# 512-column gate/up products for the first 1024 tokens with their result kept in DRAM, two down chunks per step, and a sixth seven-product unit in the sequence transform

## The chip, the cores and the metric

The kernel runs on one core of a Trainium2 chip. The metric is the device time in microseconds (us) of one execution, the median over several runs. The core has five engines that run beside one another, each with its instructions in a fixed order: TensorE (PE) multiplies, with its weight loads (PEld) overlapping; VectorE (DVE), ScalarE (ACT) and GpSimd (POOL) do elementwise work; SyncE (SP) issues the DMA transfers. An engine that waits for a semaphore holds back everything behind it in its own order.

## What is computed

One FNet block and one gated GELU block, on 2048 tokens of width 448, with a hidden width of 1792:

```python
# _A_ref: DFT over the hidden and the sequence axis, real part
a = jnp.einsum("bsd,ed->bse", x, dft_hid_re)
b = jnp.einsum("bsd,ed->bse", x, dft_hid_im)
y = jnp.einsum("ts,bse->bte", dft_seq_re, a) - jnp.einsum("ts,bse->bte", dft_seq_im, b)
...
# _B_ref
h = _gelu(g) * u            # g = x @ w_gate, u = x @ w_up
return jnp.einsum("bsf,fd->bsd", h, w_down)
...
h = x + _A_ref(_layernorm(x, axis=-1), A_dft_seq_re, A_dft_seq_im, A_dft_hid_re, A_dft_hid_im)
h2 = h + _B_ref(_layernorm(h, axis=-1), B_w_gate, B_w_up, B_w_down)
```

## The kernel before

Every operand of a product is split into two fp16 parts, a high one (written by ACT, line 106) and a low one (the rest, written by DVE, lines 110 and 112), and a product takes three terms: high by high, low by high, high by low. Many products are done by schemes with seven products of half size instead of eight; these need sums of operand blocks, which DVE or POOL make.

**Sequence transform, 0 to about 347 us.** The 16 token tiles are normalised in pairs, turned by DMA or PE, and multiplied by the hidden DFT (the feature matmuls F0 to F15, 22 of 448 columns each, into two PSUM banks `ab`, which ACT empties as the high part of `b` and DVE as the low part). Then come 8 passes p over 8 units u, each unit a block of the sequence DFT against two token tiles. A plain unit is 24 matmuls of 448 columns; a seven-product unit (its number is in `S_UNITS`) is 42 of 224 columns. The weights of a unit are loaded (`wr`), split into `ws` (`seq_parts`), and for a seven-product unit four sums are made (`wsum`: lines 518, 520 and 522, DVE) and split into `wss` (two buffers). Before, five units are of that kind and three plain.

The order on each engine in this stage is set when the kernel is built, by a planner: `arranged()` walks over tasks with a cost, a due time and the tasks they come after, and picks for each engine the earliest due task that is able to start. A table `SHIFT` moves due times by kind of task, `HOLD` lets an engine wait for a more urgent task, and `COST` has the length of a unit (plain 4.54, seven-product 4.02). Between these tasks lies the preparation of the gate/up weights: 14 groups f, each loaded (`gu_raw`), summed, split (`gu_p`) and stored to DRAM (`w_dram`). Groups in `LATE` (three before) are prepared later, during gate/up. The pass results are added to x and kept as h; layernorm of h and the operand sums of gate/up (`hops`) for the four quarters of 512 tokens follow in the same stage and beyond.

**Gate/up and down, 347 us to the end.** The tokens are in quarters of 512. A step t is one quarter q by one weight group f. With `TQ` = 256 columns it has seven products, A11B11 and A12B21 into bank pX, S2T2, S3T3 and A22T4 into pY, S1T1 and S4B22 into pZ, 39 matmuls in all (line 1199). The methods of `GateUp` (`x_open`, `x_close`, `y_mid`, `y_close`, `z_open`, `z_close`, `c_last`) issue them with the elementwise work: DVE writes hidden(1) from pZ in `y_mid` (`plus`, line 1209), hidden(0) from pY in `y_close` and `c12` from pZ in `z_close`; in `c_last` ACT applies GELU to c12 and POOL multiplies it into hidden(1) (line 1276). `z_close` adds into the bank that the plus in `y_mid` has read, and so comes after it.

A down chunk d is 21 matmuls of 224 columns (line 1144) for a part of the hidden width and of the tokens. `dn_sums` makes its sums `dn_s` (POOL: lines 1290 and 1291, DVE: 1292; `DN_S` = 3 buffers), `dn_split` its high and low parts `dn_w`. Steps 0 to 13 (the first quarter) have no chunk; each of steps 14 to 55 has one; 14 more follow at the end. The hidden values hh of a quarter stay in SBUF.

What sets the order here is the loop over t as written; the order on each engine is that of the calls. Pools that are closed and opened again (`reuse_waits="tile"`) put a wait on the first write of a new tile, for all that still uses the old ones at its place.

Of the kernel before, what the change touches and what calls it, by code (L numbers as in the profile page):

```python
# [14 lines left out]
P = 128  # L15
# [18 lines left out]
def kernel(  # L34
# [57 lines left out]
    G.memset(eps_t, EPS / X_SC**2)  # L92

# [35 lines left out]

    def root(mv, tag, of=1):  # L130
# [191 lines left out]
    S_UNITS, WR_BUFS, WS_BUFS, WSS_BUFS, STAGE_BUFS = (3, 4, 5, 6, 7), 3, 3, 2, 2
# [5 lines left out]
    xt, xs, xT, norm_x = {}, {}, {}, {}  # L328
    x_pairs = x.rearrange("(u g p) d -> u p g d", g=2, p=P)
# [93 lines left out]
    wh_hi = ring.tile([P, 4, 2 * D], F16, tag="ops", bufs=2, name="wh_hi")  # L423
    wh_lo = ring.tile([P, 4, 2 * D], F16, tag="ops", bufs=2, name="wh_lo")
# [76 lines left out]
    def sums_high(i):  # L501
        t = bop[i] = dft.tile([P, 2, 7, HD], F16, name=f"b{i}")
# [12 lines left out]
    def seq_sums(p, u):  # L515
        r = wr[p, u]
        s = wsum[p, u] = dft.tile([P, 4, 2 * P], F32, tag="wsum", bufs=1, name=f"wsum{p}_{u}")
        V.tensor_add(s[:, 0:2], r[:, 1:2].to_broadcast([P, 2, 2 * P]), r[:, 0:4:3])
        yield
        V.tensor_add(s[:, 2], s[:, 1], r[:, 0])  # L520
        yield
        V.tensor_add(s[:, 3], s[:, 2], r[:, 2])  # L522
# [39 lines left out]
    PRODUCTS = [(0, 0, 2, 0), (1, 2, 0, 1), (6, 1, 0, 0), (2, 6, 1, 1), (4, 3, 2, 1), (5, 5, 3, 0), (3, 4, 3, 1)]  # L562
# [42 lines left out]
    def seq_out(p):  # L605
# [12 lines left out]
        for g, ps in enumerate((X, Y)):  # L618
            eg = e[:, 2 * g : 2 * g + 2].rearrange("p o d -> p (o d)")
# [10 lines left out]
    class Weights:  # L630
# [52 lines left out]
        def beat(self, k):  # L683
# [31 lines left out]
    for n, s in zip((1, 3, 4, 5, 7), S_UNITS):  # L715
        mixed.insert(n, s)
# [900 lines left out]
```

## Time and profile before

| | |
|---|---|
| runs | 704.88, 705.37, 705.43 us; median 705.37 |
| the profiled execution, first to last instruction (span) | 703.5 us |
| its instructions | 15378 |
| mean granted TensorE clock | 0.999 |
| DMA over the span | 139.74 MB, mean 199 GB/s |
| sequence transform | about 0 to 347 us |
| first quarter, steps 0 to 13 | 352 to 411 us |
| steps 14 to 55 | 411 to 675 us |
| last 14 chunks | from 675 us |

The profile is of one execution. The median of the runs lies 1.87 us above its span; changes are worked out on the span and carried over to the runs. "Busy" is the time in which an engine worked on instructions. For PE it is modelled and overlaps, so it says that PE had work, not how fast: for that, starts are compared. L12 is line 12 of the kernel.

### The profile page before, as it was taken

The page shows a single profiled execution, that of the slowest core. Times are in us where ns is not written, and L with a number is a line of the kernel's source. Part 1 is how long each engine was busy: PE and PEld are TensorE (multiplying, and loading weights), DVE is VectorE, ACT ScalarE, POOL GpSimd, SP SyncE. Part 2 cuts the span into 40 slices and gives each one's busy share as a digit, 9 for nine tenths or more (in the row PEclk, how much of TensorE's full clock was granted, in tenths as well). Part 3 has the DMA queues.
Part 4 walks back from the last instruction along what each step waited for, and adds up shares of the span by engine and source line. Part 5 has one row for each costly group of instructions (what it writes and reads, how often), then busy time and mean ns, then how long its engine had stood idle before and what let it go on. Part 6 is the DMA issues. An engine that isn't in the chain of part 4 may idle for free.

```text
span 703.5 us, 15378 instructions
## 1 busy us (share of the span) xinstructions
PE 697.0 (99%) x6046; PEld 584.1 (83%) x6046; DVE 563.2 (80%) x1170; ACT 408.0 (58%) x862; POOL 198.8 (28%) x225
## 2 busy tenths in 40 slices
PE   8999999999999999999999999999999999999998
PEld 5556578878787878778888889999999999999998
DVE  6999999999999897989578877575765755786786
ACT  5776674667576565656267765555555544455432
POOL 0000000000000000001136754474664745647342
PEclk9999999999999999999999999999999999999999
DMA  9554555687988867777579665658466594545401
GB/s 330 160 128 114 142 170 184 233 245 227 228 275 202 283 177 261 262 253 281 182 258 353 204 211 170 191 180 199 170 195 190 178 200 173 181 158 166 151 27 54
DMA packets 81849, 139.74 MB, mean 199 GB/s; under 512 B 41712, under 2 KB 59376, under 8 KB 81776
## 3 DMA queue, kind: packets, MB, share of 16 engines
q1 hardware_dynamic: 81776, 138.76, 63.5%
q8 instruction: 47, 0.77, 0.5%
q14 instruction: 26, 0.21, 0.1%
HBM read 109.25 MB, written 20.19 MB: 184 GB/s over the span
## 4 chain that ended last, share of the span: by engine, by line
PE 95%; DMA 1%; ACT 1%; DVE 1%; issue 1%; SPq 0%; ACTq 0%; DVEq 0%
PE acc L574 38%; PE acc_d L1144 15%; PE pY L1199 14%; PE pZ L1199 9%; PE pX L1199 9%; PE ab L457 9%; DMA x<-in_x_dram 1%; DVE dn_w L110 0%; ACT dn_w L106 0%; SPq L429 0%; ACT xn_h L254 0%; DVE st_x L354 0%; DVE hh L1209 0%; ACT wd L106 0%; ACT g L1252 0%
## 5 line engine op out<-in xcount | busy, mean ns | idle before, releaser
L1199 PEld LDWEIGHTS <-gw 128*128 128x128 f16 x2184 | 213.1, 98 | 23.7 <-issue 1.0
L574 PE MATMUL acc<-b,ws 128*128 128x224 f16 (+1 forms) x1296 | 204.6, 301 | 0.0
L574 PEld LDWEIGHTS <-ws 128*128 128x128 f16 x1296 | 125.6, 98 | 53.2
L1199 PE MATMUL pY<-hops,gw 128*128 128x256 f16 x952 | 129.1, 273 | 0.0
L1144 PE MATMUL acc_d<-wd,dn_w 128*128 128x224 f16 x1050 | 122.3, 259 | 0.0
L574 PE MATMUL acc<-b,wss 128*128 128x224 f16 x960 | 118.2, 259 | 0.0
L235 POOL TENSOR_TENSOR wd_s<-wd 128x448 f32<-128x448 f32 x7 | 10.1, 1442 | 346.8 <-DMA wr<-in_w_seq_dram 330.0
L1144 PEld LDWEIGHTS <-dn_w 128*128 128x128 f16 x1050 | 101.1, 98 | 2.9
L574 PEld LDWEIGHTS <-wss 128*128 128x128 f16 x960 | 92.3, 98 | 0.1
L106 ACT ACTIVATE ws<-wr 128x256 f16<-128x256 f32 (+2 forms) x104 | 62.4, 637 | 41.1 <-PE acc L574 16.1
L1199 PE MATMUL pZ<-hops,gw 128*128 128x256 f16 x616 | 85.5, 273 | 0.4 <-DVE hh L1209 0.3
L1276 POOL TENSOR_TENSOR hh<-hh,c 128x256 f32<-128x256 f32 x56 | 46.3, 828 | 139.7 <-ACT c L1274 139.5
L1199 PE MATMUL pX<-hops,gw 128*128 128x256 f16 x616 | 83.3, 273 | 0.0
L112 DVE SCALAR_TENSOR_TENSOR ws<-wr,ws 128x256 f16<-128x256 f32 (+2 forms) x104 | 70.6, 709 | 1.4 <-ACT ws L106 1.3
L110 DVE TENSOR_TENSOR dn_w<-hh,dn_w 128x256 f16<-128x256 f32 x50 | 25.3, 506 | 53.1 <-ACT dn_w L106 52.8
L106 ACT ACTIVATE wss<-wsum 128x1024 f16<-128x1024 f32 x40 | 42.1, 1053 | 36.8 <-DVE wsum L522 21.1
L457 PEld LDWEIGHTS <-xT 128*128 128x128 f16 x352 | 33.9, 98 | 32.8 <-ACT xT L420 1.5
L110 DVE TENSOR_TENSOR dn_w<-dn_s,dn_w 128x640 f16<-128x640 f32 x50 | 54.6, 1092 | 7.4 <-ACT dn_w L106 6.7
L1243 ACT ACTIVATE u<-pY 128x256 f32<-128x256 f32 x56 | 21.4, 382 | 61.4 <-PE pY L1199 61.3
L1291 POOL TENSOR_TENSOR dn_s<-hh 128x256 f32<-128x256 f32 x42 | 52.8, 1258 | 0.0
L112 DVE SCALAR_TENSOR_TENSOR wss<-wsum,wss 128x1024 f16<-128x1024 f32 x40 | 48.8, 1220 | 4.1 <-ACT wss L106 4.0
L1238 ACT ACTIVATE pY<-pX 128x256 f32<-128x256 f32 x56 | 20.6, 368 | 50.3 <-PE pX L1199 50.3
(120 smaller groups left out, 936.9 us busy)
## 6 DMA issues: line engine op xcount, KB each, us to landing
gw<-w_dram SPq DMA_DIRECT2D x53, 896.0 KB, 4.8
wr<-in_w_seq_dram SPq DMA_DIRECT2D x64, 512.0 KB, 4.4
gu_raw<-in_w_gu_dram SPq DMA_DIRECT2D x28, 384.0 KB, 4.8
w_dram<-gu_p SPq DMA_DIRECT2D x33, 256.0 KB, 3.1
hx<-in_x_dram SPq DMA_DIRECT2D x8, 448.0 KB, 4.5
h_dram<-hx SPq DMA_DIRECT2D x8, 448.0 KB, 4.8
hr<-h_dram SPq DMA_DIRECT2D x8, 448.0 KB, 5.3
x<-in_x_dram SPq DMA_DIRECT2D x7, 448.0 KB, 6.9
```

The source lines that it names most:

```text
L106: A.activation(dst, src, AF.Copy, scale=scale)
L110: V.tensor_sub(dst, src, hi)
L112: V.scalar_tensor_tensor(dst, src, scale, hi, op0=ALU.mult, op1=ALU.subtract)
L235: G.tensor_sub(s[:, 2:4], t[:, 0:2], t[:, 2:4])
L457: PE.matmul(feat[i][r][:, :D], xT[i][:, kx, :], w[:, kw, r * D : (r + 1) * D], start=n == 0, stop=n == 10,)
L574: PE.matmul(banks[k][:, cols], lhs, rhs, start=k not in begun, stop=stop, skip_group_check=True)
L1144: PE.matmul(acc[k // 2][:, k % 2 * HD : (k % 2 + 1) * HD], a_of(la, a), b_of(lb, b), start=first and m == 0 and k % 2 == 0, stop=last and ...
L1199: PE.matmul(ps, w[:, wl, wa + ws, :], ops[:, m + ms, :], start=first and n == 0, stop=last and n == len(terms) - 1, skip_group_check=True,)
L1238: A.activation(self.Y, self.X, AF.Copy)
L1243: A.activation(self.u2, self.Y, AF.Copy, scale=SC)
L1276: G.tensor_mul(c22, c22, self.c12)
L1291: E.tensor_sub(s[:, 2:4], t[:, 1:4:2], t[:, 0:4:2])
```

## The change

1. `S_UNITS` gets unit 2 as well: six seven-product units and two plain ones. The blocks of a seven-product unit are renumbered so that its three plain blocks lie side by side and `seq_parts` splits them as one piece of 768 columns instead of 256 and 512. In a pass the units come in the order 0, 2, 3, 4, 1, 5, 6, 7; before, 0, 3, 1, 4, 5, 6, 2, 7.
2. The moments of the token pairs u = 7 and 4 are made by ACT (`x_moments`), and for those and for h two small steps of the reciprocal root go to ACT (`half_of` and a square).
3. The table `SHIFT` and `HOLD` have new values, with more kinds, and `LATE` has six groups instead of three: {3: 0, 5: 4, 7: 8, 9: 12, 11: 16, 13: 20}.
4. Steps 0 to 13 take the first 1024 tokens at 512 columns. Their hidden values go to `hid` tiles (4 buffers, pool scr), are stored to `hid_dram` (`store`), and are loaded as `hid_in` (6 buffers) for chunks 0 to 27. Steps 14 to 27 and 28 to 41 take the third and fourth quarter at 256 columns; there are 42 steps instead of 56. `CHUNK_COUNT` gives the chunks of steps 14 to 41, two or one; 14 follow at the end as before.
5. The product of `c_last` is a call of its own (`c_mul`), on POOL, or on DVE in steps 15 to 28. Pools are laid out anew: hh2 lies in `later`, opened when `half0` (with scr and the hid tiles) is closed in step 14.

Cut to its core:

```diff
-    S_UNITS, WR_BUFS, WS_BUFS, WSS_BUFS, STAGE_BUFS = (3, 4, 5, 6, 7), 3, 3, 2, 2
+    S_UNITS, WR_BUFS, WS_BUFS, WSS_BUFS, STAGE_BUFS = (2, 3, 4, 5, 6, 7), 3, 3, 2, 2
+    BY_SCALAR = (7, 4)
...
-            return [(w[0], slice(0, 1), r[:, 0:1]), (w[0], slice(1, 3), r[:, 2:4])]
+            return [(w[0], slice(0, 3), r[:, 1:4])]
...
-    for n, s in zip((1, 3, 4, 5, 7), S_UNITS):
+    for n, s in zip((1, 2, 3, 5, 6, 7), S_UNITS):
         mixed.insert(n, s)
...
-    SHIFT = {"copy": -31.8, "fhigh": -68.2, "fhighp": -18.1, "flow": 9.9, "fsum": 12.9, "guhi": 1.2, "gulo":
+    SHIFT = {"copy": 3226.4, "fhigh": -1619.2, "fhighp": 1413.8, "flow0": -1035.9, "flow1": -969.5,
...
-    HOLD = (0.23, 17.8)
+    HOLD = (0.24, 56.3)
...
-    LATE = {4: 0, 8: 7, 12: 15}
+    LATE = {3: 0, 5: 4, 7: 8, 9: 12, 11: 16, 13: 20}
...
+    STEPS = [(0, f) for f in range(NF)] + [(2, f) for f in range(NF)]
+    STEPS += [(3, f // 2 + f % 2 * (NF // 2)) for f in range(NF)]
...
+            self.n = 4 * P if wide else TQ
...
+            if (self.t, g) not in hid:
+                hid[self.t, g] = scr.tile([P, 4 * P], F32, tag="hid", bufs=HID_BUFS, name=f"hid{self.t}_{g}")
+            return hid[self.t, g]
+
+        def store(self, g):
+            k, n = divmod(self.f, NC)
+            nc.sync.dma_start(hid_dram[n][:, :, k, g, :], hid[self.t, g].rearrange("p (j c) -> p j c", j=4))
...
+    HID_BUFS, IN_BUFS = 4, 6
...
+    def hid_load(d):
+        p, n = divmod(d, NC)
+        hid_in[d] = early.tile([P, 4, P], F32, tag="hid_in", bufs=IN_BUFS, name=f"hid_in{d}")
+        nc.sync.dma_start(hid_in[d], hid_dram[n][:, p].rearrange("p k g c -> p (k g) c"))
...
-    N_GU = 4 * NF
+    N_GU = 3 * NF
+    ops3 = []
+    CHUNK_COUNT = (2, 2, 2, 1, 2, 2, 2, 1, 2, 2, 2, 1, 2, 2) + (2, 1) + (2, 1, 1, 1, 1, 1) * 2
...
             prev.c_last()
+            if t == NF:
+                prev.c_mul()
+                for g in range(2):
+                    prev.store(g)
+                half0.close()
+                later = ctx.enter_context(tc.tile_pool(name="later", bufs=1, side="right", reuse_waits="tile"))
+                hh[2] = later.tile([P, NC, 4, TQ], F32, name="hh2")
```

**The order at the start, DVE.** The rows follow the statistics of token pair x10, x11; `wsum0_5` is the first sum of unit 5 in pass 0, `b0` and `b1` are the low parts of the first two feature tiles (`ab0_0` is a PSUM bank), DMAHW6 the landing of wr0_5. Before:

```order
45 L354 BN_STATS st_x4_393<-x2_376 128x6 [waits DMAHW2_49]
46 L354 BN_STATS st_x5_394<-x2_376 128x6 [waits DVE_49]
47 L356 BN_AGGR mv_x4_392<-st_x4_393 128x2 [waits DVE_49]
48 L356 BN_AGGR mv_x4_392<-st_x5_394 128x2 [waits DVE_49]
49 L112 SCALAR_TENSOR_TENSOR b0_345<-ab0_0_231,b0_345 128x448 [waits Activation_49]
50 L112 SCALAR_TENSOR_TENSOR b0_345<-ab0_1_232,b0_345 128x448 [waits Activation_49]
51 L518 TENSOR_TENSOR wsum0_5_403<-wr0_5_383 128x512 [waits DMAHW6_49]
52 L112 SCALAR_TENSOR_TENSOR b1_365<-ab1_0_280,b1_365 128x448 [waits Activation_49]
```

The same place on DVE in the changed kernel:

```order
45 L549 TENSOR_TENSOR wsum0_5_395<-wr0_5_384 128x512 [waits DMAHW6_49]
46 L369 BN_STATS st_x4_398<-x2_377 128x6 [waits DMAHW2_49]
47 L369 BN_STATS st_x5_399<-x2_377 128x6 [waits DVE_49]
48 L371 BN_AGGR mv_x4_397<-st_x4_398 128x2 [waits DVE_49]
49 L371 BN_AGGR mv_x4_397<-st_x5_399 128x2 [waits DVE_49]
50 L114 SCALAR_TENSOR_TENSOR b0_346<-ab0_0_232,b0_346 128x448 [waits Activation_49]
51 L114 SCALAR_TENSOR_TENSOR b0_346<-ab0_1_233,b0_346 128x448 [waits Activation_49]
52 L114 SCALAR_TENSOR_TENSOR b1_366<-ab1_0_281,b1_366 128x448 [waits Activation_49]
```

`wsum0_5` has moved from behind b0 to ahead of the statistics of x4 and x5.

**The order from step 13 to step 14, DVE.** Rows 752 to 763 of the changed kernel; step 13 is the last wide one, and hh2 in the last row is the first write to the place that the hid tiles had; DMAHW1, 2, 6 and 7 are there the landings of the four stores of hid12 and hid13:

```order
752 L1324 SCALAR_TENSOR_TENSOR hid13_0_5745<-pY_13_5615,g1_13_5693 128x512 [waits DMAHW3_49,PE_49]
753 L1258 SCALAR_TENSOR_TENSOR c12_13_5752<-pZ_13_5638,u2_13_5651 128x512 [waits PE_49,Pool_49]
754 L112 TENSOR_TENSOR dn_w0_5758<-hid_in0_5590,dn_w0_5758 128x256 [waits Activation_49]
755 L112 TENSOR_TENSOR dn_w0_5758<-dn_s0_5671,dn_w0_5758 128x640 [waits Activation_49]
756 L112 TENSOR_TENSOR dn_w1_5763<-hid_in1_5592,dn_w1_5763 128x256 [waits Activation_49]
757 L112 TENSOR_TENSOR dn_w1_5763<-dn_s1_5675,dn_w1_5763 128x640 [waits Activation_49]
758 L1361 TENSOR_TENSOR dn_s2_5768<-hid_in2_5667 128x128 [waits DMAHW4_49]
759 L1361 TENSOR_TENSOR dn_s3_5772<-hid_in3_5669 128x128 [waits DMAHW5_49,DVE_49]
760 L114 SCALAR_TENSOR_TENSOR wd_4627<-wd_s_6_5633,wd_4627 128x1120
761 L112 TENSOR_TENSOR dn_w2_5798<-hid_in2_5667,dn_w2_5798 128x256 [waits Activation_49]
762 L112 TENSOR_TENSOR dn_w2_5798<-dn_s2_5768,dn_w2_5798 128x640 [waits Activation_49]
763 L1258 SCALAR_TENSOR_TENSOR hh2_5787<-pZ_14_5725,u3_14_5829 128x256 [waits DMAHW2_49,DMAHW6_49,DMAHW1_49,DMAHW7_49,Activation_49,Pool_49]
```

At the same place before, between the first and second quarter, DVE had less ahead of that write:

```order
748 L1209 SCALAR_TENSOR_TENSOR c12_13_5508<-pZ_13_5415,u2_13_5428 128x256 [waits PE_49,Pool_49]
749 L112 SCALAR_TENSOR_TENSOR wd_4572<-wd32_6_5317,wd_4572 128x448 [waits DMAHW5_49,Activation_49]
750 L110 TENSOR_TENSOR dn_w1_5527<-hh0_4599,dn_w1_5527 128x256 [waits Activation_49]
751 L110 TENSOR_TENSOR dn_w1_5527<-dn_s1_5378,dn_w1_5527 128x640 [waits DVE_49,Activation_49]
752 L1209 SCALAR_TENSOR_TENSOR hh1_5516<-pZ_14_5482,u3_14_5550 128x256 [waits DMAHW3_49,DMAHW1_49,Activation_49]
```

The write of step 14 now stands behind three chunks' low parts instead of one, and waits for four transfers of step 12 and 13.

**The same place, POOL of the changed kernel.** The product that finishes hid13 (the last row, L1336) stands behind the sums of chunks 2 and 3; the DVE wait of dn_s3 is for a free dn_s buffer, which the low part of chunk 0 frees:

```order
49 L1336 TENSOR_TENSOR hid12_1_5628<-hid12_1_5628,c12_12_5665 128x512 [waits DMAHW2_49,Activation_49]
50 L1359 TENSOR_TENSOR dn_s2_5768<-hid_in2_5667 128x256 [waits DMAHW4_49]
51 L1360 TENSOR_TENSOR dn_s2_5768<-hid_in2_5667 128x256
52 L1359 TENSOR_TENSOR dn_s3_5772<-hid_in3_5669 128x256 [waits DMAHW5_49,DVE_49]
53 L1360 TENSOR_TENSOR dn_s3_5772<-hid_in3_5669 128x256
54 L1336 TENSOR_TENSOR hid13_1_5715<-hid13_1_5715,c12_13_5752 128x512 [waits DMAHW7_49,DMAHW0_49,Activation_49]
```

The store of hid13_1 on SP waits for that last row. Before, the product of a step was of 256 columns and nothing was stored behind it.

More of the change, by code (lines that the diff above doesn't have):

```diff
@@ L763, in chain @@
         for k, cost in enumerate(costs):
-            last = [add(engine, cost, due, lambda k=k: step(k == 0), after=last, kind=kind)]
+            on, cost = cost if isinstance(cost, tuple) else (engine, cost)
+            last = [add(on, cost, due, lambda k=k: step(k == 0), after=last, kind=kind)]
         return last[0]
@@ L1083 @@
     gu_late(min(LATE))
+    for n in range(2):
+        down_load(n)
     h_store(N_PASS - 1)
-    down_load(1)
     banks_dft.close()
@@ L1325, in dn_drain @@
     def dn_drain(p):
-        v = [ftile(f"v{k}", 1, f"v{k}_{p}", D) for k in range(2)]
+        v = fpool.tile([P, 2, D], F32, tag="v", name=f"v_{p}")
+        v = [v[:, k] for k in range(2)]
         return Drain(hr[p], acc_d[p], v, 1.0 / (H_SC * W_SC))
@@ L1471, with some @@
             cur.z_close()
[L1472 to L1474 removed]
+            if t >= 10:
+                for d in chunks(t + 3):
+                    hid_load(d)
+            for d in chunks(t + 1):
+                dn_split(d)
+            for d in chunks(t + 2):
+                dn_sums(d)
+            do(t, 2)
+            down_end(t)
             late_prep(2 * t + 1)
+            do(t, 4)
         else:
+            mms = [(d, k) for d in chunks(t) for k in range(21)]
+            def some(a, b):
+                n = len(chunks(t))
+                for d, k in mms[a * n : b * n]:
+                    dn_mm(d, range(k, k + 1))
             do(t, 0)
             prev.c_last()
+            if t == NF:
+                prev.c_mul()
+                for g in range(2):
[3 more added lines that the diff above has]
+                hh[2] = later.tile([P, NC, 4, TQ], F32, name="hh2")
+                ops3.append(ring.tile([P, 2, N_OPS, 2 * P], F16, tag="ops", bufs=1, name="ops3"))
+                hops[3] = ops3[0][:, 0]
+            elif t > 2 * NF:
+                prev.c_mul()
+            for d in chunks(t + 3):
+                if d < 4 * NC and t + 3 < 2 * NF + 2:
+                    hid_load(d)
             cur.x_close()
@@ L1481 @@
                 cur.z_open()
-            if d + 1 < 6 * NC:
-                dn_split(d + 1)
-            dn_mm(d, range(0, 8))
-            cur.y_mid()
-            dn_ahead(t)
+            nexts = [d for d in chunks(t + 1) if d not in dn_w]
+            if t == 2 * NF - 1:
+                nexts += [d for d in chunks(t + 2) if d < 4 * NC]
+            for d in nexts[:1]:
+                dn_split(d)
+            some(0, 8)
+            if t == 2 * NF:
+                quarter2.close()
+                last = ctx.enter_context(tc.tile_pool(name="last", bufs=1, reuse_waits="tile"))
+                hh[3] = last.tile([P, NC, 4, TQ], F32, name="hh3")
+            cur.y_mid()
+            if NF < t <= 2 * NF:
+                prev.c_mul(V)
+            sums = [d for d in chunks(t + 2) if d not in dn_w]
+            if t == 2 * NF - 2:
+                sums += [d for d in chunks(t + 3) if d < 4 * NC]
+            sums = [d for d in sums if d not in dn_s]
+            for d in sums[:1]:
+                dn_sums(d)
+            for d in nexts[1:]:
+                dn_split(d)
+            for d in sums[1:]:
+                dn_sums(d)
             do(t, 6)
-            dn_mm(d, range(8, 18))
+            some(8, 18)
             if nxt:
@@ L1492 @@
             if not nxt:
-                dn_mm(d, range(18, 21))
+                some(18, 21)
             do(t, 4)
@@ L1497 @@
             if nxt:
-                dn_mm(d, range(18, 21))
+                some(18, 21)
             do(t, 5)
```

340 lines of the change are left out of this document (197 added, 143 removed).

## The prediction

> **What bounds the kernel now.** I read the busy line and the chain of waits first, then the waits of TensorE (PE), then busy time by stage, then the stretches that the change touches.
>
> ```profile
> PE 697.0 (99%) x6046; PEld 584.1 (83%) x6046; DVE 563.2 (80%) x1170; ACT 408.0 (58%) x862; POOL 198.8 (28%) x225
> PE 95%; DMA 1%; ACT 1%; DVE 1%; issue 1%; SPq 0%; ACTq 0%; DVEq 0%
> ```
>
> PE is busy for 697.0 of 703.5 us and makes up 95% of the chain that ends last. The waits of PE (total, times, longest) say how little there is to win by removing one:
>
> ```profile
> PE pw L100 <- POOL eps_t L92: 1.4, 1, 1.4
> PE ab L457 <- ACT xT L420: 0.4, 1, 0.4
> ...
> PE pZ L1199 <- DVE hh L1209: 0.3, 1, 0.3
> ```
>
> Next, busy time by stretch of the span; after the length come PE, PEld, DVE, ACT and POOL, then the granted clock, the share of the DMA engines and GB/s:
>
> ```profile
> 60.00:200.00 140.00, 140.00 (x1115) 107.34 (x1114) 131.97 (x259) 93.85 (x166) 0.00 (x0) 1.00 0.68 201
> 200.00:347.00 147.00, 147.00 (x1233) 118.38 (x1231) 128.97 (x257) 85.97 (x164) 4.77 (x3) 1.00 0.77 246
> 352.00:411.00 59.00, 58.98 (x542) 52.72 (x540) 47.16 (x83) 40.96 (x99) 33.54 (x34) 1.00 0.76 264
> ```
>
> PE is full in every stretch at full clock; VectorE (DVE) is the next one, 94% and 88% busy in the two sequence stretches. So the kernel gains by what is taken off PE, unless DVE or a transfer then comes late.
>
> **What a matmul costs.** A modelled end hides the true pitch, so I count from start to start in the order of time of PE (start, length, what, count):
>
> ```profile
> 23.45 2.81 PE L457 MATMUL ab<-wh_hi,xT 128*128 128x448 f16 x14
> 26.09 1.68 PE L457 MATMUL ab<-wh_lo,xT 128*128 128x448 f16 x8
> 27.61 3.57 PE L574 MATMUL acc<-b,ws 128*128 128x448 f16 x18
> ```
> ```profile
> 149.77 0.55 PE L574 MATMUL acc<-b,ws 128*128 128x224 f16 x4
> ...
> 153.60 2.62 PE L574 MATMUL acc<-b,ws 128*128 128x448 f16 x13
> ```
> ```profile
> 400.75 1.36 PE L1199 MATMUL pX<-hops,gw 128*128 128x256 f16 x11
> 401.95 0.82 PE L1199 MATMUL pY<-hops,gw 128*128 128x256 f16 x6
> ```
>
> 448 columns: 14 in 2.64 us, 188.6 ns. 224 columns: a sequence unit of seven products has 42, the two that precede 149.77 apart, and the 40 from 149.77 take 3.83 us: 95.75 ns. 256 columns: 11 in 1.20 us, 109.1 ns. The slope between 224 and 448 is 0.4145 ns a column, so 512 columns, of which the trace has none, should take 188.6 + 64 x 0.4145 = 215.1 ns, an estimate. If it took twice the 256 (218.2) nothing would be saved.
>
> **Part 1, one more seven-product unit (u = 2), in all 8 passes.** Each pass loses 24 matmuls of 448 columns and gains 42 of 224: 24 x 188.6 - 42 x 95.75 = 4526 - 4022 = 505 ns. Times 8: **-4.0 us** on PE, on the path.
>
> What DVE pays for it, by form (busy, mean ns | idle before):
>
> ```profile
> L518 DVE TENSOR_TENSOR wsum<-wr 128x512 f32<-128x512 f32 x40 | 28.4, 709 | 9.0 <-DMA wr<-in_w_seq_dram 8.8
> L520 DVE TENSOR_TENSOR wsum<-wsum,wr 128x256 f32<-128x256 f32 x40 | 16.8, 419 | 0.3
> L112 DVE SCALAR_TENSOR_TENSOR wss<-wsum,wss 128x1024 f16<-128x1024 f32 x40 | 48.8, 1220 | 4.1 <-ACT wss L106 4.0
> L112 DVE SCALAR_TENSOR_TENSOR ws<-wr,ws 128x1024 f16<-128x1024 f32 x24 | 29.7, 1238 | 1.0 <-ACT ws L106 0.9
> L112 DVE SCALAR_TENSOR_TENSOR ws<-wr,ws 128x512 f16<-128x512 f32 x40 | 27.3, 684 | 0.1
> L106 ACT ACTIVATE wss<-wsum 128x1024 f16<-128x1024 f32 x40 | 42.1, 1053 | 36.8 <-DVE wsum L522 21.1 <-PE acc L574 7.0 <-DVE r_h L148 4.1
> ```
>
> A seven-product unit costs DVE 0.71 + 2 x 0.42 for the sums, 1.22 for their low part and about 1.0 for the low part of its plain blocks (now one piece of 768 columns, between the 684 of 512 and the 1238 of 1024): 3.8 us, a plain unit 1.24. Over the stage, counted by instructions: sums +12, their low parts +10, plain low parts -8 (the merging pays for more than it adds), the two more tiles of features with sums +4. Against it go three weight groups moved out into gate/up, 24 instructions of mostly 0.4 to 0.7 us like
>
> ```profile
> L112 DVE SCALAR_TENSOR_TENSOR gu_p<-gu_s,gu_p 128x512 f16<-128x512 f32 x22 | 16.0, 726 | 0.0
> ```
>
> (-14), and the moments of two pairs with 18 small steps, which ACT takes (-6). Net about -2 us, while PE takes 4 less, and DVE idles 26 of the 287 us in the first two windows above. I take zero for this stage. What hides the added work is DVE's lead over PE, and at the tightest spot it is small: the sums' tile has two buffers, so a third such unit in a row waits for the end of the first and then has 4.02 us for 1.05 (ACT) + 1.22 (DVE), some 1.7 us of slack. If that cover goes, that unit is late (the slower rival).
>
> **Part 2, products of 512 columns for the first 1024 tokens.** 14 steps x 39 products stand in place of 28 x 39 of 256 columns: 546 x (218.2 - 215.1) = **-1.7 us**. Ends: 0 (512 costs twice 256) and about -3 (the estimate off by as much the other way). The weights of these 14 groups are read once instead of twice, and 28 results of 256 KB are stored and read back instead: DMA runs at 264 GB/s in 352 to 411 now, my sum for the wide steps is about 250 GB/s. Per wide step of 8.4 us I count about 5.8 us of DVE and 5 of ACT; neither binds. The down chunks move two to a step but their number and columns are the same: zero on PE. The three weight groups moved here lie in those wide steps, under 2.6 us of DVE reserve a step.
>
> **Part 3, the start.** In DVE's order the first sum of the first seven-product unit (wsum0_5, L518) moves ahead of the statistics of x4, x5 and the low parts b0, b1. It waits for the load of wr0_5. DVE by time now, the issue of that load (SPq) and the time from issue to landing of the only wr load in that window:
>
> ```profile
> 11.75 0.43 SPq L513 DMA_DIRECT2D wr<-in_w_seq_dram  x1
> ```
> ```profile
> wr<-in_w_seq_dram SPq DMA_DIRECT2D x1, 512.0 KB, 10.3
> ```
> ```profile
> 20.70 1.12 DVE L354 BATCH_NORM_STATS2 st_x<-x 128x6 f32<-128x448 f32 x2
> 21.73 0.30 DVE L356 BATCH_NORM_AGGREGATE mv_x<-st_x 128x2 f32<-128x6 f32 x2
> 21.95 1.12 DVE L112 SCALAR_TENSOR_TENSOR b<-ab,b 128x448 f16<-128x448 f32 x2
> 22.99 0.68 DVE L518 TENSOR_TENSOR wsum<-wr 128x512 f32<-128x512 f32 x1
> 23.59 1.15 DVE L112 SCALAR_TENSOR_TENSOR b<-ab,b 128x448 f16<-128x448 f32 x2
> ...
> 25.52 1.23 DVE L112 SCALAR_TENSOR_TENSOR ws<-wr,ws 128x1024 f16<-128x1024 f32 x1
> ```
>
> The load lands at 11.75 + 10.3 = 22.05. So DVE, free at 20.70, idles to 22.1, sums to 22.7, does the statistics to 23.95 and b0 to 25.05, 2.1 us later than now. Behind b0 stands F3 on PE, whose bank b0 empties: it starts at 23.45 now (the quoted row, right behind the first half of b0) and would start at about 24.65, its second bank at 25.15. F3 ends 29.1 instead of 27.6. DVE goes on with b1 (26.05), twelve small steps instead of six (27.2), then b2 ahead of ws0_0 (28.25), and ws0_0 ends 29.5; the first plain unit reads it at its third matmul. **+1.6 us**: from 1.0 (the load lands at 21.5) to 2.0. The rest of this stage starts that much later and nothing in it can be brought forward, PE being full.
>
> **Part 4, from the last wide step (13) to the first narrow one (14).** hh2 lies where the hid tiles of the wide steps lay, so its first write by DVE (the first plus of step 14) waits until the last stores of hid12 and hid13 have landed; before, the analogous write of hh1 had a short wait. Rows for the chain (POOL is GpSimd), and the store of nearest size:
>
> ```profile
> L110 DVE TENSOR_TENSOR dn_w<-hh,dn_w 128x256 f16<-128x256 f32 x50 | 25.3, 506 | 53.1 <-ACT dn_w L106 52.8
> L110 DVE TENSOR_TENSOR dn_w<-dn_s,dn_w 128x640 f16<-128x640 f32 x50 | 54.6, 1092 | 7.4 <-ACT dn_w L106 6.7
> L1290 POOL TENSOR_TENSOR dn_s<-hh 128x256 f32<-128x256 f32 x42 | 38.4, 913 | 0.0
> L1291 POOL TENSOR_TENSOR dn_s<-hh 128x256 f32<-128x256 f32 x42 | 52.8, 1258 | 0.0
> L1276 POOL TENSOR_TENSOR hh<-hh,c 128x256 f32<-128x256 f32 x56 | 46.3, 828 | 139.7 <-ACT c L1274 139.5
> L112 DVE SCALAR_TENSOR_TENSOR wd<-wd_s,wd 128x1120 f16<-128x1120 f32 x7 | 9.2, 1314 | 0.0
> ```
> ```profile
> w_dram<-gu_p SPq DMA_DIRECT2D x33, 256.0 KB, 3.1
> ```
>
> I count from the end of step 13's last product on PE. DVE writes c12_13 until 0.95 (PE's latency 0.3, 512 columns by the 709 of L518), then the low parts of chunk 0 (0.45 + 1.0): 2.35. Only then is a dn_s buffer free, so POOL's two sums for chunk 3 run 1.5 to 2.2 us: 4.0 to 4.6. Behind them stands the product that finishes hid13, 512 columns: 1.3 to 1.65 us, to 5.3 to 6.3. Its store of 256 KB needs about 3.1 us: landed 8.5 to 9.8. hh2 follows, and PE's last product of step 14, which adds to the bank that hh2 reads, may begin at 9.0 to 10.2. Without waiting PE is there at 36 x 95.75 ns (two chunks to piece 18) + 22 x 109.1 ns = 5.85. The wait is 3.2 to 4.3 us. What before loses at its own place is taken off:
>
> ```profile
> 419.12 0.71 PE L1199 MATMUL pY<-hops,gw 128*128 128x256 f16 x5
> 420.12 0.71 PE L1199 MATMUL pZ<-hops,gw 128*128 128x256 f16 x5 [0.29 <-DVE hh L1209]
> ```
>
> Five products after 419.12 end at 419.67, the next starts at 420.12: 0.45. I take **+3.3 us**. The least is set by DVE alone, whose queue ahead of hh2 holds, after c12_13, the low parts of chunks 0, 1 and 2 (3 x 1.6), two small sums (under 0.42 each, as L520) and wd's 1.31: 7.9, and with a plus of 0.4 some 8.3, or +2.0. These means hold time in which POOL ran beside DVE, so I put the least at +1.4; the most, +4.5, has store and product slower than their rows. PE and DVE both have reserve in step 15, so nothing more follows.
>
> **The sum.** -4.0 - 1.7 + 1.6 + 3.3 = -0.8 us on the profiled span of 703.5: 702.7. The median of the runs, 705.37, lies 1.87 above that span; with it 704.6 us.
>
> **Rivals.** *Faster:* the stores land before DVE arrives and the start costs 1.0: -4.0 - 1.7 + 1.0 + 1.4 = -3.3, 702.0 us; with the wait at half of my figure still under 703.9. For it speaks that POOL's rows are rough; against, that dn_s of chunk 3 cannot start ahead of DVE's low parts. *Slower:* DVE falls behind in the rows of three seven-product units that the new order makes twice a pass. There it has 3 x 3.8 = 11.4 us of their own work in 12.1 us, so a drain of 2 us or a weight group that falls into such a row pushes the sums' low part past its 1.7 us. It decides once that piece ends more than 4.0 us after the unit two ahead has ended; 0.5 us in each of 7 passes gives +3.5, 708.1. For it speaks DVE's 131.97 of 140 us; against, that it idles 9.0 us for the loads alone ahead of L518, work it could have taken. *The clock:* in step 14 PE stops for 3 to 4 us, longer than anywhere in this trace after the start. After the idle start it was slow (min/median/max of a warm-up matmul, first and last start):
>
> ```profile
> L100 PE MATMUL pw<-ident x50: 219/314/315, 1.4 to 6.4; 128*128 128x128 f16 x50
> ```
>
> At 314 instead of 219 ns for 5 us PE would lose 5 x (1 - 219/314) = 1.5 us, once: 706.1. The Trainium skill, TensorE: Matmul & The Clock Gate, section "What's actually happening", has the clock halved after an idle window of 3.4 us that runs freely; by that, a stop barely as long seldom covers a whole window, and half the clock for the next 3.4 us would cost 1.7. *The width:* wider products might hide their weight load and get cheaper per column, all in part 2: at the 188.6 of 448 columns it would save at most 546 x (218.2 - 188.6) = 16.2 us, 690 us. The rows speak against it: from 224 to 448 columns each added column costs the same. The same page, section "Back-to-back issue gap", gives 131 ns sustained for 512 columns; by that the change would save 48 us, and the trace, with 188.6 ns for 448 with a weight load before each, disagrees. *Nothing of it:* that the units or the widths stay as they were is excluded by the code.
>
> **How the numbers follow.** 0.2% of 705.37 is 1.4 us, about what can be told from no change: faster is below 703.96, slower above 706.78. My forecast's case, with start 1.0 to 2.0 and step 14 1.4 to 4.5, reaches from 702.1 to 706.2: chance 0.62, of which 0.19 lies below 703.96 (a step-14 loss under 2.7) and 0.43 inside the 0.2%. The faster rival has 0.11, the slower one 0.17, the clock 0.08 (0.05 of it joined with a long wait, above 706.78), the width 0.02. Faster: 0.19 + 0.11 + 0.02 = 0.32; slower: 0.17 + 0.05 = 0.22; same: 0.43 + 0.03 = 0.46. The range 702.0 to 707.7 holds the forecast's case, the clock, half of the slower rival and most of the faster one.
>
> **What would show it.** In the changed profile: the units' 42 matmuls in 4.02 us; 512 columns at 215 ns from start to start; DVE idle some 1.4 us before wsum near 21, and the first sequence matmul near 29.2; PE waiting 3 to 4 us for hh at the end of step 14, with POOL's last product of hid13 ending over 5 us after step 13. Waits of acc on wss in the passes would make it wrong upward; an hh wait below 1.5 us, downward.

## The result, and the profile after

The changed kernel takes 723.16 us (median of 4 runs, 720.39 to 723.51) against 705.40 for the kernel before: ratio 1.0236, 95% interval 1.0215 to 1.0257. Run again with the last experiments, the ratio was 1.0226 (1.0206 to 1.0245). The forecast was 704.6, no change. The profiled execution has a span of 721.3 us, 17.8 more than before. Two runs far off the others, of 1219 and 1884 us, one each of two kernels below, are in none of the medians.

The busy line and the chain of waits of the changed kernel:

```profile
PE 698.2 (97%) x5644; PEld 547.0 (76%) x5644; DVE 588.4 (82%) x1112; ACT 415.0 (58%) x800; POOL 168.2 (23%) x198
PE 69%; issue 9%; DVE 8%; POOL 5%; DMA 4%; ACT 4%; SPq 0%; POOLq 0%; DVEq 0%; ACTq 0%
```

PE has 402 fewer matmuls, as the change makes it (546 fewer in the wide steps, 144 more in the passes), but it is 69% of the chain where it was 95%. The waits of PE name where it went (total, times, longest):

```profile
PE pZ L1248 <- DVE c L1258: 8.1, 7, 2.2
PE pZ L1248 <- DVE hh L1258: 6.6, 1, 6.6
PE pw L102 <- POOL half_eps L94: 1.4, 1, 1.4
PE acc L605 <- DVE wss L114: 1.2, 1, 1.2
PE xT_ps L445 <- DVE xs L112: 1.1, 2, 0.9
PE acc_d L1190 <- DVE dn_w L112: 0.9, 1, 0.9
```

Only the second of these has a term in the forecast's sum; the fourth, on wss, is what its slower rival was about. The first, seven waits on c12, was in none of its cases. By stretch (length; PE, PEld, DVE, ACT and POOL busy; granted clock; DMA share; GB/s):

```profile
60.00:200.00 140.00, 140.00 (x1177) 113.24 (x1176) 131.94 (x226) 91.64 (x145) 0.00 (x0) 1.00 0.59 172
352.00:461.00 109.00, 109.00 (x506) 49.32 (x505) 80.94 (x130) 65.17 (x117) 40.34 (x35) 1.00 0.77 234
470.00:480.50 10.50, 3.95 (x39) 3.60 (x38) 6.59 (x8) 2.29 (x5) 6.55 (x7) 0.86 0.58 166
480.50:484.00 3.50, 3.44 (x18) 2.54 (x18) 2.21 (x8) 1.41 (x2) 0.83 (x2) 0.50 0.55 153
490.00:600.00 110.00, 104.69 (x999) 97.52 (x997) 76.15 (x157) 51.21 (x126) 49.88 (x66) 0.98 0.61 191
600.00:700.00 100.00, 97.10 (x935) 90.35 (x933) 77.73 (x142) 47.27 (x119) 56.71 (x64) 1.00 0.39 135
```

The part of the sequence stage shown (first row) and the wide steps (second) are full, on the terms forecast. Most of the loss begins where wide meets narrow (third row), is followed by 3.5 us at half the clock (fourth), and goes on through the narrow steps (fifth and sixth), where PE misses 5.3 and 2.9 us although DVE is busy for only 69% and 78% of the time. That last point is what the experiments had to explain: a wait for an engine that is not full.

### The profile page after: what moved, and what is told of

Its sections match the earlier page's. It is cut to its first block, busy times and chain, and to the rows that moved or that the text cites. A ratio compares the mean times of both kernels' runs of the same rounds, so it can differ in the third digit from the quotient of the medians.

```text
span 721.3 us, 14527 instructions
## 1 busy us (share of the span) xinstructions
PE 698.2 (97%) x5644; PEld 547.0 (76%) x5644; DVE 588.4 (82%) x1112; ACT 415.0 (58%) x800; POOL 168.2 (23%) x198
## 4 chain that ended last, share of the span: by engine, by line
PE 69%; issue 9%; DVE 8%; POOL 5%; DMA 4%; ACT 4%; SPq 0%; POOLq 0%; DVEq 0%; ACTq 0%
PE acc L605 33%; PE acc_d L1190 13%; PE ab L484 9%; PE pY L1248 7%; PE pZ L1248 5%; PE pX L1248 4%; DVE dn_w L112 2%; DMA hid_dram<-hid 2%; POOL hid L1336 1%; POOL wd_s L251 1%; DVE dn_s L1361 1%; DMA wr<-in_w_seq_dram 1%; POOL wd_s L249 1%; DMA x<-in_x_dram 1%; POOL wd_s L252 1%
## 5 line engine op out<-in xcount | busy, mean ns | idle before, releaser
L1248 PEld LDWEIGHTS <-gw 128*128 128x128 f16 x1638 | 160.9, 98 | 92.6 <-issue 16.9
L605 PE MATMUL acc<-b,wss 128*128 128x224 f16 x1152 | 141.9, 259 | 1.2 <-DVE wss L114 1.2
L1248 PE MATMUL pY<-hops,gw 128*128 128x512 f16 (+1 forms) x476 | 89.9, 328 | 0.1
L108 ACT ACTIVATE ws<-wr 128x768 f16<-128x768 f32 (+1 forms) x64 | 56.3, 888 | 26.5 <-PE acc L605 12.4
L1248 PE MATMUL pZ<-hops,gw 128*128 128x512 f16 (+1 forms) x308 | 59.7, 328 | 11.9 <-DVE hh L1258 6.6
L484 PE MATMUL ab<-wh,xT 128*128 128x448 f16 x352 | 70.1, 358 | 0.5 <-DMA xT<-xs 0.2
L114 DVE SCALAR_TENSOR_TENSOR ws<-wr,ws 128x768 f16<-128x768 f32 (+1 forms) x64 | 64.9, 1018 | 0.0
L1248 PE MATMUL pX<-hops,gw 128*128 128x512 f16 (+1 forms) x308 | 57.1, 326 | 0.0
L1181 POOL TENSOR_TENSOR hr<-hr,v 128x224 f32<-128x224 f32 x56 | 41.3, 761 | 12.3 <-ACT v L1149 11.9
L108 ACT ACTIVATE dn_w<-dn_s 128x640 f16<-128x640 f32 x50 | 36.5, 730 | 8.5 <-DVE dn_s L1361 8.5
```

Source lines behind the costliest of these rows:

```text
L108: A.activation(dst, src, AF.Copy, scale=scale)
L114: V.scalar_tensor_tensor(dst, src, scale, hi, op0=ALU.mult, op1=ALU.subtract)
L484: PE.matmul(feat[i][r][:, :D], xT[i][:, kx, :], w[:, kw, r * D : (r + 1) * D], start=n == 0, stop=n == 10,)
L605: PE.matmul(banks[k][:, cols], lhs, rhs, start=k not in begun, stop=stop, skip_group_check=True)
L1181: op(x, x, m)
L1248: PE.matmul(ps, w[:, wl, wa + ws, :], ops[:, m + ms, :], start=first and n == 0, stop=last and n == len(terms) - 1, skip_group_check=True,)
```

## The experiments

Each experiment has its own runs of the kernel before beside it, whose medians lie between 705.63 and 707.08 us. So kernels are compared by their ratios to it, and waits by their traces.

**Step 14 alone: hh2 in seven tiles.** Cut to its core; the places that read and write hh2 follow.

```diff
-                hh[2] = later.tile([P, NC, 4, TQ], F32, name="hh2")
+                hh[2] = {n: later.tile([P, 4, TQ], F32, name=f"hh2_{n}") for n in range(NC)}
```

> hh2 is made of seven tiles (one per n) in place of one, so that the first write of step 14 lies where nothing of the hid tiles was and waits for no store. Reading of the profile after: PE waits 6.6 us for that write, until 480.56, and the next products run slow. Theory A (the landing of the stores is what ends last): the write moves up to the end of DVE's own queue, the low part that ended at 476.17, so PE goes on at about 476.6: 4.0 us gained, and up to 1.8 more if the slow clock behind the wait goes: 717.3 to 719.2. Rival B (DVE's queue is nearly as late and takes over): under 1.5 us gained, 721.7 or more.

Measured 716.38 us, ratio 1.0137 (1.0118 to 1.0156): some 1% better, a little more than theory A said. The wait fell from 6.6 to 2.6 us, and those 4.0 us are the edit's. The rest of the gain is not: in this execution the clock did not fall behind the later stop of 2.2 us, and the first sequence product started 0.8 us earlier. Behind the stop in step 14 the clock still fell. What bounds that wait now is DVE's own queue, as theory A had it:

```profile
PE pZ L1248 <- DVE c L1258: 7.8, 7, 2.2
PE pZ L1248 <- DVE hh L1258: 2.6, 1, 2.6
```

**Step 14 again: only the order of the transfers.**

```diff
-        ahead = {0: (), 11: (14,), 12: (), 13: (15,), 14: (16,)}.get(t, (t + 3,) if t < NF else (t + 2,))
+        ahead = {0: (), 11: (14,), 12: (), 13: (15,), 14: ()}.get(t, (t + 3,) if t < NF else (t + 2,))
...
                     prev.store(g)
+                gw_load(16)
                 half0.close()
```

> hh2 is one tile as in the changed kernel, but the load of gw16 (896 KB) is issued behind the last two hid stores instead of ahead of them. Theory A1 (the stores of hid13, 7.3 us from issue to landing, share the DMA engines with gw16): they land within 3.1 to 4.2 us, at about 476 to 477, and the gain is that of the seven tiles or up to 1 us less: 717.5 to 720. Rival A2 (stores in pieces of 512 bytes are slow by themselves): landing still after 6 us or more, gain under 1.5 us, 721.7 or more.

Measured 718.04 us, ratio 1.0158 (1.0138 to 1.0178), and the same wait of 2.6 us. The DMA issues between 470 and 473 us in the changed kernel (KB each, median us from issue to landing):

```profile
gw<-w_dram SPq DMA_DIRECT2D x1, 896.0 KB, 7.6
hid_dram<-hid SPq DMA_DIRECT2D x2, 256.0 KB, 7.4
hid_in<-hid_dram SPq DMA_DIRECT2D x1, 256.0 KB, 4.4
```

and, in this kernel, between 465 and 476 us:

```profile
gw<-w_dram SPq DMA_DIRECT2D x1, 896.0 KB, 5.0
hid_in<-hid_dram SPq DMA_DIRECT2D x3, 256.0 KB, 3.3
hid_dram<-hid SPq DMA_DIRECT2D x2, 256.0 KB, 3.2
```

The same store takes 7.4 us behind a load of 896 KB that was issued 1 us earlier, and 3.2 ahead of it: theory A1. Pieces of 512 bytes are not what made it slow.

**The narrow steps: the product into pZ later.**

```diff
-            if t > NF:
-                cur.z_open()
...
             some(0, 8)
+            if t > NF:
+                cur.z_open()
```

> In steps 15 to 41 the first product into pZ (z_open) comes behind the first 8 of 21 pieces of the down chunks instead of ahead of them. PE has eight waits there (steps 19, 22, 23, 26, 33, 35, 37, 39), 9.5 us together, for c12 of the step before, which stands in DVE's queue behind the splits, sums and side work. Theory C (c12 is late by that much, and PE only needs other work meanwhile): 1.53 us more in a two-chunk step and 0.77 in a one-chunk step cover 7.5 of the 9.5; with the slow clock behind two of them 7 to 9 us gained: 714 to 716. Rival D (DVE is overloaded over several steps, so the wait comes back one product later, at the write of hh in y_mid): 0 to 3 us gained, 720 or more.

717.28 us, ratio 1.0146 (1.0121 to 1.0170), between the two forecasts. The waits on c12 nearly go, but others come, as rival D had it, though at another place than it said: at the down products into an accumulator whose banks are drained late (by DVE, line 1153, and ACT, line 1149). PE's waits from 482 to 700 us:

```profile
PE acc_d L1190 <- DVE hr L1153: 2.9, 2, 1.5
PE acc_d L1190 <- ACT v L1149: 1.8, 5, 0.4
PE pZ L1248 <- DVE c L1258: 0.6, 2, 0.4
```

8.1 us became 5.3. So giving PE other work only shows the next thing that stands behind the same queues.

**The product on POOL.** `prev.c_mul(V)` behind `y_mid` in steps 15 to 28 becomes `prev.c_mul()` at the start of the step, as in the later steps.

> The product that finishes hidden(1) in steps 15 to 28 goes back from DVE to POOL, as in steps 29 to 41. Theory C (c12 waits for a full DVE queue): 0.42 us less of DVE ahead of c12 in each of steps 18, 21, 22, 25, the waits of steps 19, 22, 23, 26 shrink by 0.4 each or somewhat less since POOL and DVE slow each other: 0.5 to 2 us gained, 721 to 722.7. Rival E (POOL then becomes the late one, as its sums stand behind the product): 1 us or more lost, above 724.

718.87 us, ratio 1.0171 (1.0150 to 1.0192): about 4 us better than the changed kernel by the ratios, more than theory C said, and rival E is out. Where the gain lies stays open.

**The second split in its own step.**

```diff
+            for d in chunks(t)[1:]:
+                if d not in dn_w:
+                    dn_split(d)
...
+            elif t != 2 * NF - 2:
+                nexts = nexts[:1]
```

> Of the changed kernel one thing is moved: in steps 15 to 41 the split of a step's second down chunk (ACT and DVE, 1.25 us of DVE alone and about 2.15 us beside POOL) is issued at the start of its own step instead of in the step before. A one-chunk step, 6.3 us on PE, then prepares one chunk and not two. Theory C' (the waits for c12 come from one-chunk steps in which DVE has 8 us of work or more): the 9.5 us of waits at steps 19 to 39 shrink below 3.5, 6 to 8 us gained with the slow clock behind the longest: 714.5 to 717.5. Rival D (DVE is short over the whole stretch): the waits come back in the two-chunk steps, under 2.5 us gained, 720.5 or more.

719.84 us, ratio 1.0194 (1.0169 to 1.0219), between the two forecasts. Waits on c12 fall to 4.5 us, halfway. Of the 5.3 us at steps 19 to 26, 0.4 is left, at step 23; 0.9 comes at step 27, which had none; and those of steps 33 to 39 stay (2.8 us before, 3.1 now, with one of 0.3 at step 37). Theory C' explains the first group only.

**Five seven-product units.** `S_UNITS` (3, 4, 5, 6, 7) and the old places in the pass.

> The changed kernel with five seven-product units instead of six (units 3 to 7; order in a pass 0, 3, 1, 4, 5, 6, 2, 7), everything else as changed; the planner makes its order anew. By the prediction's part 1, PE has 4.0 us more to do; the wait for the low part of the sums at 242 us (1.35) may go, so 2.7 to 4.0 us lost: 725.5 to 727.5. Rival (the sixth unit costs in DVE what it saves on PE, or disturbs the gate/up stage through the weight groups): no change within 1 us, or a gain.

732.73 us, ratio 1.0384 (1.0353 to 1.0415), far outside both. The planner, with its table meant for six units, makes an order in which PE waits once for 6.9 us early on, and then runs at half the clock:

```profile
PE ab L484 <- DVE b L114: 6.9, 1, 6.9
```

This does not measure the unit, and is no verdict on it; both forecasts are left undecided. What it is worth is read from the passes instead, below.

**The moves put together.** hh2 in seven tiles and the second split in its own step; in addition the small root steps go from step 13 to 16, and the last wd low part and the split of chunk 2 go behind the first write of hh2.

> Together: hh2 in seven tiles, the second split in its own step, and around step 14 three pieces of DVE work moved back: the small steps of the last h root from step 13 to 16, the last down weights' low part and the split of chunk 2 behind the first write of hh2. By the parts: the wait of 6.6 us in step 14 falls to under 1.5, the 1.1 us at its first chunk goes, 6 to 8 us come from the second split, and the slow clock behind the long waits (3 us together) goes: 705 to 708.5. Rival (these waits share a cause, DVE's sum over steps 13 to 28, and only move): 711 or more.

712.48 us, ratio 1.0088 (1.0063 to 1.0114): a little beyond the rival's bound. Of the 8.1 us on c12, 6.7 are left, 2.1 of them new, at step 15, behind the moved wd part.

> As the kernel with the three moves, and the product that finishes hidden(1) in steps 15 to 28 on POOL instead of DVE. If DVE is still what waits are for: 1 to 3 us less than the three moves. If POOL becomes late: 1 us or more above.

711.40 us, ratio 1.0077 (1.0049 to 1.0105), no different from the one before within the intervals; the waits on c12 are 6.3 us instead of 6.7.

**The order on DVE: side work behind c12.** Until here c12 was looked at as the victim of too much work. Of step 38 in the last kernel, DVE's order of time (start, length) shows something else:

```profile
659.14 0.41 DVE L1258 SCALAR_TENSOR_TENSOR hh<-pZ,u 128x256 f32<-128x256 f32 x1
659.47 0.48 DVE L1365 TENSOR_TENSOR dn_s<-hh 128x128 f32<-128x128 f32 x1
659.87 0.87 DVE L1363 TENSOR_TENSOR dn_s<-hh 128x256 f32<-128x256 f32 x1
660.67 0.88 DVE L1364 TENSOR_TENSOR dn_s<-hh 128x256 f32<-128x256 f32 x1
661.47 0.74 DVE L1365 TENSOR_TENSOR dn_s<-hh 128x128 f32<-128x128 f32 x1
662.14 0.41 DVE L1326 SCALAR_TENSOR_TENSOR hh<-pY,g 128x256 f32<-128x256 f32 x1
662.47 0.41 DVE L1258 SCALAR_TENSOR_TENSOR c<-pZ,u 128x256 f32<-128x256 f32 x1
664.00 0.48 DVE L112 TENSOR_TENSOR dn_w<-hh,dn_w 128x256 f16<-128x256 f32 x1 [1.12 <-ACT dn_w L108]
```

Three us of sums, needed a step later at the earliest, run ahead of hh and c12, and right behind c12 DVE idles 1.12 us. So two kernels were made in which this work, and the preparation of the last quarter's operands, is issued behind c12 (a new place, 8). The first is built on the one above; in it the wd part goes behind c12 as well, and the second split is late only up to step 25. Cut to its core:

```diff
-                (1, 1, lambda q=q, j=j: ffn_sums(q, j, (0,))),
+                (1, 8, lambda q=q, j=j: ffn_sums(q, j, (0,))),
...
-        at(side, (t, 6), lambda n=n: dn_sums(6 * NC + n, V))
+        at(side, (t, 8), lambda n=n: dn_sums(6 * NC + n, V))
...
             do(t, 3)
+            do(t, 8)
```

> The three moves with the product on POOL, and DVE's side work of steps 14 to 41 (operand sums and low parts of the last quarter, sums of the last chunks, the down weights' last low part) is issued behind c12 of its step instead of ahead of it; the second split is late only up to step 25. Theory F (it is the order: c12 stands behind work that nothing waits for yet): of the 9 us of waits that are left from step 15 on (2.3 at step 15, 1.2 at 27, 5.0 at 33 to 39) 6 us or more go, and the slow clock behind the one at step 15 (1.3): 6 to 8 us less than the kernel before this one, 703 to 706. Rival D (DVE and POOL slow each other and DVE is short over these stretches): 2 us less or nothing, 709 or more.

705.68 us, ratio 0.9984 (0.9967 to 1.0000): theory F. PE's waits from 490 to 700 us, 8.1 us in the changed kernel, are now

```profile
PE pZ L1248 <- DVE c L1258: 0.7, 1, 0.7
PE acc_d L1190 <- ACT v L1149: 0.7, 1, 0.7
PE pZ L1248 <- DVE hh L1258: 0.3, 1, 0.3
```

> Of the changed kernel only the place of DVE's side work of steps 14 to 41 is moved behind c12 of its step; splits, hh2 and the rest as changed. Theory F (order): the waits at 19, 22, 23, 26 lose what stood ahead of c12 (0.3 to 1.5 us each) and those at 33, 35, 37, 39 go: 9.5 falls to 3 to 4, 5 to 7 us gained, 716 to 718. Rival C' (the second split alone decides): under 3 us gained, 720 or more.

Alone, on the changed kernel, it gives 717.03 us, ratio 1.0142 (1.0115 to 1.0170), inside theory F:

```profile
PE pZ L1248 <- DVE hh L1258: 4.8, 1, 4.8
PE pZ L1248 <- DVE c L1258: 3.5, 4, 2.0
```

PE waits 3.5 us for c12 in four places instead of 8.1 in seven, and not at all after step 28. At step 22 the wait stays (2.0 us, before 1.6): there the second split still stands ahead. The 1.8 us by which the wait on hh is shorter are not the edit's; in the second run of the changed kernel it was 5.6 us.

**The rest, and the changed kernel again.** In the sequence stage, wss goes ahead of the weight sums that stand directly before it on DVE; the last wd part goes behind the last quarter's normalisation; the drains of the first three accumulators end a step earlier (`n // 2 * 2` in place of `n`).

> The kernel with side work behind, and three more places: in the sequence stage the low part of the sums (wss) goes ahead of weight-group sums that stand directly before it on DVE; the down weights' last low part in step 14 goes behind the last quarter's normalisation, for which ACT waited; the sums of the drains end one step earlier. If the wait of 1.35 us at 242 us has the cause that the order shows (two weight sums, 0.97 us, ahead of wss), it falls to 0.4 or less; the 1.3 us at 479 and the 0.8 at 531 go: 2.5 to 3.1 us less than with side work behind, ratio to before 0.994 to 0.996. If DVE only loses them elsewhere: no change, 0.997 or more.

> As the kernel with the low part of the sums first, but with the planner's order in the sequence stage left alone. If that move is worth what the wait at 242 us shows: 0.9 to 1.35 us slower than with it. If it costs other waits: equal or faster.

Both 704.29 us, ratio 0.9972 (0.9961 to 0.9983, and 0.9958 to 0.9986). The wait on wss is 0.4 us with the move and 0.9 without it, but the times do not tell the two apart, and the 0.994 to 0.996 expected of the first was missed. They are the only versions whose whole interval lies below the kernel before, by 0.28%; the span of the first is 700.7, PE 99% busy again.

> The changed kernel itself, beside the others on this chip. Theory G (the start's loss hangs on when the second x load lands: a gap on PE of 1.1 us or more before 8 us lets the clock fall, a shorter one does not): if the trace shows a gap under 1.0 us, the first sequence product starts by 28.0 us and the span is 1 to 2 us under 721.3; if it shows 1.1 or more, some ten matmuls of 448 columns at 374 ns follow and it starts after 28.6. If the slow matmuls come without such a gap, G falls.

Ratio 1.0226, span 719.1. The waits in the narrow steps are the same to the tenth (8.1 us, 7 times), the one on hh 5.6. On its start, below.

## Why the prediction was wrong

**Part 1, the unit: right.** Starts of one pass (first product) and of the next, before and then after:

```profile
178.78 1.49 PE L574 MATMUL acc<-b,ws 128*128 128x448 f16 x7
212.53 2.25 PE L574 MATMUL acc<-b,ws 128*128 128x448 f16 x11
```
```profile
178.78 1.49 PE L605 MATMUL acc<-b,ws 128*128 128x448 f16 x7
212.01 2.81 PE L605 MATMUL acc<-b,ws 128*128 128x448 f16 x14
```

33.75 us became 33.23: 0.52, forecast 0.505. The cover that it named, DVE's lead, held except at one place, at 243 us, where wss came 1.2 us late (0.7 in the second run); so the slower rival had its place, once instead of seven times.

**Part 2, the width: right in the products.** Eleven products of 512 columns, from start to start:

```profile
401.04 2.54 PE L1248 MATMUL pX<-hops,gw 128*128 128x512 f16 x11
403.41 0.81 PE L1248 MATMUL pY<-hops,gw 128*128 128x512 f16 x3
```

215.5 ns, forecast 215.1. The width rival, and the 131 ns of the Trainium skill (TensorE: Matmul & The Clock Gate, "Back-to-back issue gap"), are out; that section's formula for a product by itself gives 216 for 512 and fits this stream.

**The step that failed is in part 2:** "The down chunks move two to a step but their number and columns are the same: zero on PE." The columns are the same, but the work ahead of c12 on DVE is not. A one-chunk step takes 6.3 us on PE and prepared two chunks. In step 25 DVE's order up to c12, for which the first product into pZ of the next step waits until 575.78, is this:

```profile
569.93 0.42 DVE L1258 SCALAR_TENSOR_TENSOR hh<-pZ,u 128x256 f32<-128x256 f32 x1 [0.32 <-ACT u L1307]
570.27 0.42 DVE L1336 TENSOR_TENSOR hh<-hh,c 128x256 f32<-128x256 f32 x1
570.62 0.81 DVE L1361 TENSOR_TENSOR dn_s<-hid_in 128x128 f32<-128x128 f32 x1
571.35 0.88 DVE L112 TENSOR_TENSOR dn_w<-hid_in,dn_w 128x256 f16<-128x256 f32 x1
572.15 1.27 DVE L112 TENSOR_TENSOR dn_w<-dn_s,dn_w 128x640 f16<-128x640 f32 x1
573.35 0.28 DVE L1361 TENSOR_TENSOR dn_s<-hid_in 128x128 f32<-128x128 f32 x1
573.55 1.51 DVE L112 TENSOR_TENSOR xs<-tt,xs 128x64 f16<-128x64 f32 x2
574.99 0.41 DVE L1324 SCALAR_TENSOR_TENSOR hh<-pY,g 128x256 f32<-128x256 f32 x1
575.32 0.41 DVE L1258 SCALAR_TENSOR_TENSOR c<-pZ,u 128x256 f32<-128x256 f32 x1
```

With the first split ahead of these rows, from 568.16, it needs 7.6 us to the end of c12, of which the second split (571.35 and 572.15) is 2.15 and side work (xs) 1.5. Right before 568.16 DVE stands idle for 1.8 us, for ACT's high part of the first split; so an engine that is not full makes PE wait. Whether that part could come earlier was not tried.

"PE and DVE both have reserve in step 15, so nothing more follows" made the same mistake: I had summed DVE's work over whole steps and never asked what stands ahead of c12.

The price was 8.1 us by the waits and 9.5 by the starts (the sum of the eight stops over the usual pitch). The second split explains most of the part up to step 26 (with it in its own step 5.3 us fell to 0.4, though 0.9 came at step 27), and the order of the side work explains the part from step 33 on (2.8 us, none left with that order alone). With both changed, 0.7 us is left; that kernel also has the product on POOL, which by itself changed the waits on c12 little, from 6.7 to 6.3.

**Part 4, step 14: right in place, mis-sized.** POOL's last product of hid13 ended 6.0 us after step 13, inside the 5.3 to 6.3. But its store took 7.4 us where I had 3.1, a median over stores of earlier stages that asks nothing about the load ahead; the term, +3.3 net, was 6.3 (6.77 by the starts, less 0.46 before). Ahead of it chunk 0's low part cost another 1.1, in no term: the small root steps on DVE ahead of it, two of which took 0.74 and 0.65 us while POOL worked, put it late.

**The clock: given 0.08, and it came.** After the stop of 6.6 us, PE had clock 0.50 in the window 480.5 to 484, and by the starts some 1.8 us of work was lost. The forecast had 1.5, from a smaller slowdown (314 to 219 ns) over a longer time, so that the sizes agree is partly luck. It came a second time behind a stop of 2.2 us, which I had not thought long enough:

```profile
575.70:579.20 3.50, 3.42 (x22) 2.83 (x22) 2.53 (x7) 1.62 (x4) 0.75 (x2) 0.61 0.96 322
```

Read in tenths of a us, the granted clock of this execution is 0.50 from 9.9 to 13.3, from 477.5 to 484.3 and from 576.5 to 579.9: 3.4, 6.8 and 3.4 us, and the starts lie 137 and 29 times 3.41 us apart. So the clock changes on a grid. The stop of 2.2 us (573.6 to 575.8) lies inside one stretch of it. In the kernel with hh2 in seven tiles the same stop (567.9 to 570.1) left the clock alone, 1.00 in 566 to 574; counted on from its own slow stretch, which begins at 476.0, a boundary falls at about 568.1 (an estimate) and cuts that stop. The Trainium skill, TensorE: Matmul & The Clock Gate, "What's actually happening", has a window of 3.4 us that runs freely: the lengths (6.8 is two of them) and the grid agree. It lets the clock fall after an idle window, and that a whole window must be idle does not agree: 2.2 us inside one were enough.

**Part 3, the start: about the size, by luck.** The first sequence product started at 28.78 instead of 27.61. DVE did not idle before wsum: the wr load landed early, at 20.5. In that execution the second x load landed at 6.8 us instead of 5.5, PE stopped for 0.9 us longer, and the clock fell. The window from 9.4 to 13.2 us in the changed kernel, and in its second run, in which that load landed at 6.0:

```profile
9.40:13.20 3.80, 3.73 (x14) 1.77 (x14) 2.92 (x9) 2.75 (x5) 0.00 (x0) 0.56 1.05 417
```
```profile
9.40:13.20 3.80, 3.21 (x22) 1.56 (x20) 2.96 (x7) 3.10 (x6) 0.00 (x0) 1.00 1.05 417
```

Without the slow clock, in that second run, the start is 28.28, 0.7 later than before: there DVE idles 0.65 us for the wr load (forecast 1.4), F3 starts 0.5 late and its second bank 0.34. Eight of the kernels above, with the same order at the start and no slow clock, start at 27.57 to 28.00, 0 to 0.4 us later than before. So the order that part 3 priced at 1.0 to 2.0 us cost 0 to 0.7; that term was mis-sized, and the 1.2 of the profiled execution came with the slow clock. The expectation for the second run, 28.0, was missed by 0.3. That the clock falls behind a gap of 1.1 us or more and not behind a shorter one held in the traces looked at, with a thin margin: it fell behind waits of 0.91 us and, with only the side work moved, 1.05, and not behind one of 0.86.

The sum by the starts of PE's matmuls: -5.5 for the products, +1.5 start (with 0.37 at 33 us), +1.5 wss, +1.2 chunk 0, +6.3 hh, +9.5 c12, less 0.8 of such stops before, +3.4 slow clock at 480 and 576: 17.1 of 17.8 us. The rest is not assigned.

## What to carry to other kernels

Where one engine is the bound and a second one feeds it, count for every instruction that the bound engine waits on what is queued ahead of it in that very step; a share of busy time over a stage, or even a step, cannot show it. If work is bundled unevenly, two to a step and then one, look at the step with the least time and the most preparation. Work that nothing waits for yet belongs behind the instruction that frees the next bank. That change of order, with no work removed, took the ratio from 1.0236 to 1.0142 alone, and from 1.0077 to 0.9984 on top of the other moves; of this the waits on c12 are 4.6 and 5.6 us.

When a tile takes the place of others that are still being stored, cut it so that its first part lies elsewhere, and issue large loads behind the store that is waited for.

## What the runs showed that was not expected

A 256 KB store took 7.4 us behind an 896 KB load and 3.2 us ahead of it. The same sums on DVE ran twice as long while POOL worked: dn_s of 128x256 took 0.87 and 0.88 us in the rows of step 38 above, beside POOL, and 0.41 each a step later (666.40 and 666.73 in the same trace), when POOL was idle. And the clock can fall behind stops of 0.9 to 2.2 us, for 3.4 us at half.
